# Attention into two MoE layers on one core: queries and keys in longer runs, one merged chain, a later fourth weight sum

## The chip, the cores and the metric

The kernel runs on one core of a Trainium2 chip. The metric is device time in microseconds (us). TensorE (PE in the profile) multiplies matrices; VectorE (DVE), ScalarE (ACT) and GpSimd (POOL) work on rows of elements; SyncE (SP) issues transfers, which 16 DMA engines carry out. Each engine works through its own list of instructions in order, and semaphores hold it where another engine's result is needed.

## What is computed

Attention of 4 batches, 8 heads, 576 tokens of 64 elements: a mean-pooled attention (four tokens to one, result repeated four times) plus a local one in which a token sees only its neighbours at a distance below 4. The 2304 tokens of 512 then go through two layers of an expert with 2048 inner units.

```python
def _attn_ref(q, k, v):                    # q, k, v: [4, 8, 576, 64]
    q_d = q.reshape(B, H, Sd, factor, D).mean(axis=3)          # factor 4; k_d, v_d too
    out_up = np.repeat(sm_attn(q_d, k_d, v_d), factor, axis=2)
    mask = np.abs(pos[:, None] - pos[None, :]) < factor
    scores = np.where(mask, scale * q @ k.T, -1e9)
    out_local = softmax(scores) @ v
    return out_up + out_local

def _moe_ref(x, w_in, w_out):              # [2304,512], [512,2048], [2048,512]
    h = x @ w_in
    return np.maximum(0.01 * h, h) @ w_out

def _moe2_ref(x, w_in, w_out):             # same shapes
    h = x @ w_in                           # 0 below -1, h above 1, (h+1)**2/4 between
    g = np.where(h >= 1, h, np.where(h <= -1, 0, (h + 1) ** 2 / 4))
    return g @ w_out
```

## The kernel before

**The list planner.** The program is written as chains of operations, each with an engine, a planned duration and what it depends on. A list planner (class Issue, from L165) walks through planned time and gives each engine the ready operation of least rank, subject to free memory, free PSUM banks and each chain's due step. The result is fixed at build time: on the chip every engine works down its list and waits on semaphores. In the first 140 planned microseconds (FILL), whenever the planned TensorE has nothing ready, or the planner counts too little streamed by it of late, it places a **filler**: a matmul of zeros with 512 columns whose result nobody reads (fill(), L2301).

**Attention.** P_BLOCKS names the blocks of 64 tokens whose local attention runs on TensorE: all nine of batch 0, seven of batch 1. The others go over VectorE (local_d). For each of the four head pairs of those two batches, prep() loads q and k (L957): two DMAs each, one per head, in which one element run is a token's 64 floats (256 bytes). The tile holds 64 partitions (the token within its block) by nine blocks; TensorE transposes each block of 64x128 (L992, five blocks and then four), and ScalarE copies the transposed columns out of PSUM into qT and kT, contiguous (L1005). down() does the pooled attention (its sums over four tokens, L1079 and beside; a product on GpSimd, L1061). local_p() is the chain of the local attention: a matmul that lays the mask into PSUM (L1262, or L1268 where the piece is the last block), the scores (L1277), row maximum (DVE L1290), exp (ACT L1295), the norm (L1302, L1303, L1313), the transposes (L1320), a copy (ACT L1324), the product with v (L1337), the sum with the pooled part (DVE L1351) and its split into two f16 numbers (ACT L1361, DVE L1367). Batch 0 has pieces of 4, 4 and 1 blocks, batch 1 of 3 and 4, each for four head pairs.

**The layers.** Weights arrive as 64-bit numbers (DMAs of 512 KB and more), are rebuilt to f32 on VectorE (L628, L634, L640) and split into a high and a low f16 part (ACT L662, DVE L695); every product is three matmuls. Tokens come in four blocks of 512 and one of 256. L1698 is the first product of a block, L1961 and L1973 the second. In the second layer the last three blocks use seven products of halves in place of eight (L1727, L1897), for which sums of quarters of the weights are made: out_sums() makes four (T1 to T4) for every two slices of w_out, in one chain: VectorE sums rows of 1024 (L771), combines them at 512 (L782), ScalarE makes the high part (L802) and VectorE the low one (L805). EARLY_O says how many of these chains may run before the first layer's weight memory is handed over.

Of the kernel before, what the change touches and what calls it, by code (L numbers as in the profile page):

```python
# [9 lines left out]
F16 = mybir.dt.float16  # L10
# [20 lines left out]
LEAD_O = 4  # L31
# [6 lines left out]
FP = 2  # L38
EARLY_O = 2
# [32 lines left out]
LO_PE = (0, 0)  # L72
ADD_PE = ()
# [13 lines left out]

NORM_ACT = (1,)
# [269 lines left out]
def kernel(  # L358
# [103 lines left out]
    ident_w = const.tile([P, P], F32, name="ident_w")  # L462
    ident_n = const.tile([P, P], F16, name="ident_n")

    def consts():
# [4 lines left out]
        nc.vector.tensor_scalar_mul(ident_w, ident, SW)  # L470
        nc.vector.tensor_scalar_mul(ident_n, ident, -1.0)
# [103 lines left out]
    def weight(m, which, f, due):  # L575
# [89 lines left out]
        if m == 1 and f < LO_PE[which]:  # L665

            def low():
                ps = st["ps"] = banks.get()
                nc.tensor.matmul(ps, ident_w, st["f", f].ap, start=True, stop=False)
                nc.tensor.matmul(ps, ident_n, hi, start=False, stop=True)  # L670

            ch.op("PE", dict(dur=5 * t_mm(512), cols=5 * 512), low, banks=1, mlp=True,
                  after=free)
            w_ready[m, which, f] = ch.op(
                "ACT", t_act(512, True), lambda: nc.scalar.copy(lo, st["ps"]),
                after=(lambda: banks.put(st["ps"]),))
            ch.close()
            return
# [62 lines left out]

    FH = KFF // 2
# [10 lines left out]
    def half_sums(ch, size, row, own, steps, groups, deps, need, last=(), gate=None):  # L753
# [20 lines left out]
        for i in order:  # L774
            made[i] = ch.op(
                "DVE", t_dve(size), lambda i=i: rebuild(i, i == order[0]), deps,
                need=(size,) + (need[:1] if i == order[0] else ()))
# [78 lines left out]
    def out_sums(f, due):  # L856
        words = 3 * FP * HD
        keep = {}
        fs = range(f, f + FP)

        def make():
            b = buf(words)
            keep["a"] = b.ap.bitcast(F16).rearrange("p (j s f n) -> p j s f n", j=3, s=2, f=FP)
            for k, g in enumerate(fs):
                o_ap[g] = {nm: keep["a"][:, j, :, k] for j, nm in enumerate(("T1", "T4", "T2"))}
                o_ap[g]["T3"] = w2_out[:, :, g, HD:2 * HD]

        ch = Chain(due, LEAD_O, 4 * FP * HD)
        ch.window = WINDOW_O
        r = half_sums(  # L870
            ch, 2 * FP * HD,
            lambda i: w2_out[:, :, f + FH * (i - 1):f + FH * (i - 1) + FP], "T", T_STEPS,
            ((("11",), ("T1",), lambda s: keep["a"][:, 0, s]),
             (("21", "22"), ("T4", "T2"), lambda s: keep["a"][:, 1:3, s]),
             (("12",), ("T3",), lambda s: w2_out[:, s, f:f + FP, HD:2 * HD])),
            [w_ready[2, 1, g + k] for g in fs for k in (0, FH)], (words, make),
            [o for g in fs for o in o_after.get(g, [])], lambda: f < EARLY_O or w1_open())
        for g in fs:
            o_ready[g] = r
# [65 lines left out]
    def prep(b, hp, due):  # L945
# [6 lines left out]

        def load(nm, src):
            st[nm] = buf(QBB * P, True)
            a = st[nm].ap[:QB].rearrange("p (n h d) -> p n h d", n=QBB, h=2)
            for par in range(2):
                nc.sync.dma_start(  # L957
                    out=a[:, :, par, :],
                    in_=src[b, 2 * hp + par].rearrange("(n i) d -> i n d", i=QB),
                )  # L960
# [35 lines left out]
        def tr_c(nm, i):  # L996
# [3 lines left out]
            if i == 0:  # L1000
                t.make()
                if nm == "k":
                    nc.gpsimd.memset(t.ap[:, 0:HALO], 0.0)
                    nc.gpsimd.memset(t.ap[:, S + HALO:], 0.0)
            nc.scalar.activation(  # L1005
                out=t.ap[:, o + n0 * QB:o + n1 * QB],
                in_=st["ps", nm, i][:, :(n1 - n0) * QB],
# [1329 lines left out]
```

## Time and profile before

| | us |
|---|---|
| median of 3 runs (836.97 to 837.43) | 837.23 |
| profiled execution | 837.84 |
| its span, first to last instruction | 836.1 |
| TensorE busy | 829.8 |
| VectorE busy | 704.7 |
| ScalarE busy | 439.2 |
| GpSimd busy | 44.0 |

The profiled execution has its own time, 837.84 us; 1.74 us of it lie outside the span. A busy share is an average over stages: in the first 100 us attention and the first layer run side by side, later the layers alone. A filler counts as busy TensorE, so a busy TensorE in the first 140 us is not always useful work.

### The profile page before, as it was taken

Reading aid. Unit: us, or ns where it says so; the run is one execution under the profiler, and the core shown is the slowest. Engines: PE = TensorE matmul, PEld = TensorE weight load, DVE = VectorE, ACT = ScalarE, POOL = GpSimd, SP = SyncE. Lnnn points to the kernel's source line nnn. Section 1 sums busy time; section 2 is a strip of 40 time slices with the busy share of each in tenths; the row PEclk is TensorE's granted clock in tenths of the full one; section 3 lists DMA queues with packets and bytes.
Section 4 is the critical chain, followed back from the end, with each engine's and each line's share of the span. In section 5 each row is a group of like instructions: output and inputs, shape, how many; then the busy total and the mean of one; then the engine's idle time right before and its main releaser. Section 6 shows DMA issues by size and latency. Waiting matters only on the chain.

```text
span 836.1 us, 15212 instructions
## 1 busy us (share of the span) xinstructions
PE 829.8 (99%) x5818; PEld 501.4 (60%) x5818; DVE 704.7 (84%) x1298; ACT 439.2 (53%) x1055; POOL 44.0 (5%) x64
## 2 busy tenths in 40 slices
PE   9999999999999999999999999999999999999998
PEld 5665554444444444554444444444588888889997
DVE  4997999899999999748996989997598988867761
ACT  4888874454345334644353322344365777766650
POOL 2201000000000022100330000000000000000000
PEclk9999999999999999999999999999999999999999
DMA  7879565457640244411563030000000000000001
GB/s 141 171 180 232 175 200 208 137 165 223 224 139 2 66 111 65 94 57 58 104 118 114 1 111 3 1 1 2 1 1 1 2 1 2 26 15 13 3 14 64
DMA packets 77991, 67.82 MB, mean 81 GB/s; under 512 B 36318, under 2 KB 65374, under 8 KB 77918
## 3 DMA queue, kind: packets, MB, share of 16 engines
q1 hardware_dynamic: 66718, 62.69, 26.0%
q0 software_dynamic: 11200, 4.15, 4.5%
q8 instruction: 46, 0.75, 0.4%
q14 instruction: 27, 0.22, 0.1%
HBM read 62.08 MB, written 4.72 MB: 80 GB/s over the span
## 4 chain that ended last, share of the span: by engine, by line
PE 98%; ACT 1%; DVE 0%; issue 0%; DVEq 0%
PE bank L1698 32%; PE bank L1961 22%; PE bank L1897 11%; PE bank L1727 11%; PE bank L1973 10%; PE bank L2301 3%; PE bank L992 1%; PE bank L1277 1%; PE bank L1187 1%; PE bank L1118 1%; PE bank L1337 1%; PE bank L1169 1%; PE bank L1320 1%; PE bank L1553 1%; PE bank L1262 0%; PE bank L1102 0%
## 5 line engine op out<-in xcount | busy, mean ns | idle before, releaser
L1698 PE MATMUL bank<-arena,w 128*128 128x512 f16 (+1 forms) x1344 | 285.1, 364 | 0.0
L1698 PEld LDWEIGHTS <-w 128*128 128x128 f16 x1344 | 130.2, 98 | 135.2 <-issue 1.6
L1961 PE MATMUL bank<-arena,w 128*128 128x512 f16 (+1 forms) x816 | 181.8, 373 | 0.0
L1961 PEld LDWEIGHTS <-w 128*128 128x128 f16 x960 | 93.1, 98 | 88.2 <-issue 0.2
L1810 ACT ACTIVATE arena<-bank 128x512 f32<-128x512 f32 x64 | 38.1, 595 | 97.8 <-PE bank L1698 92.4
L1973 PE MATMUL bank<-w,arena 128*128 128x512 f16 x384 | 88.2, 379 | 0.0
L1940 DVE SCALAR_TENSOR_TENSOR arena<-arena 128x512 f16<-128x512 f32 x96 | 66.0, 687 | 22.3 <-ACT arena L1936 22.0
L1936 ACT ACTIVATE arena<-arena 128x512 f16<-128x512 f32 x96 | 60.4, 630 | 36.9 <-DVE arena L1822 33.6
L1973 PEld LDWEIGHTS <-arena 128*128 128x128 f16 x384 | 36.8, 98 | 43.2 <-issue 1.2
L1897 PEld LDWEIGHTS <-w 128*128 128x128 f16 x516 | 50.3, 98 | 5.7
L1727 PEld LDWEIGHTS <-w 128*128 128x128 f16 x576 | 48.8, 98 | 4.4
L1814 ACT ACTIVATE arena<-bank,half 128x512 f32<-128x512 f32 x36 | 24.7, 687 | 42.2 <-PE bank L1698 38.5
L1547 DVE TENSOR_TENSOR arena<-arena 128x768 f32<-128x768 f32 (+2 forms) x60 | 41.2, 688 | 1.4
L662 ACT ACTIVATE w<-arena 128x512 f16<-128x512 f32 x34 | 21.3, 627 | 37.0 <-DVE arena L640 36.8
L1472 DVE TENSOR_TENSOR arena<-arena 128x1792 f32<-128x1792 f32 x20 | 40.3, 2019 | 0.3 <-issue 0.3
L1517 DVE TENSOR_TENSOR arena<-arena 128x1792 f32<-128x1792 f32 x20 | 40.3, 2017 | 0.0
L1480 DVE TENSOR_REDUCE arena<-arena 128x28 f32<-128x1792 f32 x20 | 40.2, 2013 | 0.1
L1727 PEld LDWEIGHTS <-arena 128*128 128x128 f16 x432 | 36.7, 98 | 5.3 <-issue 1.9
L1897 PE MATMUL bank<-w,w 128*128 128x256 f16 x300 | 38.6, 273 | 0.0
L1822 DVE SCALAR_TENSOR_TENSOR arena<-arena,bank 128x512 f32<-128x512 f32 x36 | 24.6, 683 | 16.5 <-ACT arena L1818 16.4
L1822 DVE SCALAR_TENSOR_TENSOR w<-w,bank 128x512 f32<-128x512 f32 x36 | 24.6, 684 | 14.4 <-ACT w L1818 14.1
L1727 PE MATMUL bank<-w,w 128*128 128x128 f16 (+1 forms) x384 | 35.9, 246 | 0.0
(199 smaller groups left out, 1290.2 us busy)
## 6 DMA issues: line engine op xcount, KB each, us to landing
arena<-in_moe_w_in_dram SPq DMA_DIRECT2D x18, 512.0 KB
arena<-in_moe_w_out_dram SPq DMA_DIRECT2D x17, 512.0 KB
w<-in_moe_w_out_dram SPq DMA_DIRECT2D x15, 512.0 KB
arena<-in_moe_w_in_dram SPq DMA_DIRECT2D x4, 1024.0 KB
w<-in_moe_w_in_dram SPq DMA_DIRECT2D x3, 1024.0 KB
arena<-in_k_dram SPq DMA_DIRECT2D x23, 112.0 KB
arena<-in_v_dram SPq DMA_DIRECT2D x23, 112.0 KB
out_dram<-arena SPq DMA_DIRECT2D x10, 256.0 KB
```

The lines of the kernel that those rows point to most:

```text
L1472: nc.vector.tensor_tensor(pv(par, j0), st["q", par].ap.rearrange("p (j d) -> p j d", d=D)[:, j0:j0 + JC, :] .unsqueeze(2).to_broadcast([P, ...
L1480: nc.vector.reduce_sum(sv(par)[:, j0:j0 + JC, :], pv(par, j0), axis=AX)
L1517: nc.vector.tensor_tensor(pv(par, j0), window(st["v", par], j0, JC), sv(par)[:, j0:j0 + JC, :].unsqueeze(3).to_broadcast([P, JC, W, D]), o ...
L1547: nc.vector.tensor_tensor(out, x, y, op=ALU.add)
L1698: nc.tensor.matmul(h[:, e], a[:, f, c, :], y[:, :, c, :], start=(n == 0), stop=(n == 3 * KDM - 1),)
L1727: nc.tensor.matmul(o[:, e], a[:, i, c], y[:, k, c, :], start=first and e == 0 and n == 0, stop=n == 5, skip_group_check=True,)
L1822: nc.vector.scalar_tensor_tensor(out=t, in0=t, scalar=1.0 / s_in, in1=st["h", p], op0=ALU.min, op1=ALU.max)
L1897: nc.tensor.matmul(o[:, k], a[:, i, at:at + P], y[:, j], start=opens and p == e == k == n == 0, stop=p == PH - 1 and e == E - 1 and n == 2 ...
L1936: nc.scalar.activation(out=gv(p)[0], in_=st["t", p].ap, func=AF.Copy, scale=so)
L1940: nc.vector.scalar_tensor_tensor(out=lo, in0=st["t", p].ap, scalar=so, in1=hi, op0=ALU.mult, op1=ALU.subtract)
L1961: nc.tensor.matmul(o, a, y[:, e, :], start=(first and n == 0 and c % E == 0), stop=(last and n == 2), skip_group_check=True,)
L1973: nc.tensor.matmul(st["acc"][tt], a, y[:, f, :], start=(first and n == 0), stop=(last and n == 2),)
```

## The change

Line numbers of the changed kernel stand in brackets.

- **q and k of batches 0 and 1** (TURN): one DMA loads q or k of a head pair [L1040]. Partition i holds tokens 9i to 9i+8 of each head, one run of 2304 bytes. 32 transfers of 144 KB become 16 of 288 KB. GpSimd copies the tile into the order that the transposes read [L1049], in two parts of 5 and 4 blocks (64 partitions by 640 and 512 floats). A transposed block n now holds tokens n, n+9, n+18, ..., so ScalarE's copy out of PSUM [L1102] writes with a step of nine floats (36 bytes). The planned costs of the load are smaller, and 1.3 us of GpSimd are planned per q or k.
- **Batch 0's last block:** four chains of one block (one per head pair) become one chain of four; it needs one mask matmul, one row maximum, one norm, one copy and so on, over four blocks' columns.
- **w_out's sums:** out_sums makes T1, T2 and T3 in one chain [L883, L891, L894, L921, L923] and T4 in a second one that is due eight steps later [L934, L944, L946, L948]. EARLY_O goes from 2 to 4 (two chains may run early instead of one), and memory is set aside for the coming x2 pairs when a chain starts (Kept).
- Paths that were switched off (LO_PE, ADD_PE) and two constants that only they used (ident_w, ident_n) are gone.

The planner then places everything anew, as order shows. There are 61 fillers in place of 86: 16 in place of 18 ahead of the first transposes, 45 in place of 68 after that. The layers' matmuls are the same.

GpSimd ahead of its first product for the pooled attention; w_61 is the memory of the early work, L1003 and L1004 clear the edges of kT. Before:

```order
L486 MEMSET arena 128x3
L487 MEMSET arena 128x3
L967 MEMSET w_61 3x64
L1003 MEMSET w_61 128x3
L1004 MEMSET w_61 128x3
L1061 TENSOR_TENSOR w_61<-w_61 72x4x128
```

After:

```order
L1059 MEMSET w_61 3x64
L1049 COPY w_61<-w_61 64x2x5x64 x2
L1049 COPY w_61<-w_61 64x2x4x64
L1049 COPY w_61<-w_61 64x2x5x64
L1095 MEMSET w_61 128x3
L1096 MEMSET w_61 128x3
L1049 COPY w_61<-w_61 64x2x4x64
L1049 COPY w_61<-w_61 64x2x5x64
L1049 COPY w_61<-w_61 64x2x4x64 x2
```

The copies of the first two head pairs stand ahead of the first product; 32 of them are on GpSimd's list in all.

TensorE, the last block of batch 0 (L1268 is its mask, L1277 its scores). Before, two of the four chains:

```order
L1268 LDWEIGHTS ident_72
L1268 MATMUL bank_70<-band,ident_72 128x70
L1277 MATMUL bank_70<-w_61 64x70 x2
L1187 MATMUL bank_69<-w_61 64x144 x4
L1320 MATMUL bank_66<-ident,w_61 70x128 x4
L1268 LDWEIGHTS ident_72
L1268 MATMUL bank_64<-band,ident_72 128x70
L1277 MATMUL bank_64<-w_61 64x70 x2
```

After, all four head pairs under one mask (scores at L1386):

```order
L1381 LDWEIGHTS ident_72
L1381 MATMUL bank_68<-band,ident_72 128x280
L1386 MATMUL bank_68<-w_61 64x70 x4
L1386 MATMUL bank_68<-arena,w_61 64x70 x2
L1386 MATMUL bank_68<-w_61 64x70 x2
L2402 LDWEIGHTS zeros
L2402 MATMUL bank_63<-zeros 128x512
L1290 MATMUL bank_64<-arena,w_61 64x144 x4
```

Three masks with their weight loads are gone, and one bank is in use where four were.

TensorE, transposes of five blocks of a q or k of batch 1 beside the first layer (L992, now L1084). Before, at about 78 us, fillers (L2301) stand around them:

```order
L2301 MATMUL bank_67<-zeros 128x512
L992 MATMUL bank_67<-ident,w_61 128x64 x5
L1169 MATMUL bank_63<-ident,w_61 72x72 x4
L2301 LDWEIGHTS zeros
L2301 MATMUL bank_65<-zeros 128x512
```

After, matmuls of the layer (L1797 was L1698, L2060 was L1961) stand around them:

```order
L1797 MATMUL bank_63<-arena,w_79 128x512
L1429 MATMUL bank_67<-ident,w_61 70x128 x4
L1084 MATMUL bank_69<-ident,arena 128x64 x5
L2060 LDWEIGHTS w_79
L2060 MATMUL bank_68<-arena,w_79 128x512
```

The diff, cut to its core:

```diff
-EARLY_O = 2
+T4_LATE = 8.0
+KEEP = 2
+EARLY_O = 4
...
+RUSH_M = 8.0
+TURN = (0, 1)
+T_LOAD = 0.7
+L_LOAD = 1.2
+T_TURN = 1.3
...
     def out_sums(f, due):
...
+        ch = Chain(due, LEAD_O, 3 * n)
+        a = ch.op("DVE", t_dve(2 * n), row, [w_ready[2, 1, g + k] for g in fs for k in (0, FH)],
+                  need=Kept((2 * n, 2 * n, n)))
+        b = ch.op("DVE", t_dve(n), last_q, [a], need=(n,))
+        t1 = ch.op("DVE", t_dve(n), lambda: minus(lambda: r(0), lambda: r(1), lambda: r(0)), [a])
+        t3 = ch.op("DVE", t_dve(n), lambda: minus(lambda: r(1), q22, lambda: r(1)), [b, t1])
+        t2 = ch.op("DVE", t_dve(n), lambda: minus(q22, q22, lambda: r(0)), [t3])
...
+        ch = Chain(due + T4_LATE, LEAD_O, 2 * n)
+        o = ch.op("DVE", t_dve(2 * n), diff, [ready["T2"]], need=Kept((n, 2 * n)))
...
         def load(nm, src):
...
+            st["r", nm] = buf(QBB * P, True)
+            nc.sync.dma_start(
+                out=st["r", nm].ap[:QB].rearrange("p (h x) -> p h x", h=2),
+                in_=src[b, 2 * hp:2 * hp + 2].rearrange("h (i n) d -> i h (n d)", n=QBB),
+            )
+
+        def turn(nm, i):
+            n0, n1 = ((0, NA), (NA, QBB))[i]
+            if not i:
+                st[nm] = buf(QBB * P, True)
+            nc.gpsimd.tensor_copy(
+                st[nm].ap[:QB].rearrange("p (n h d) -> p h n d", n=QBB, h=2)[:, :, n0:n1],
+                st["r", nm].ap[:QB].rearrange("p (h n d) -> p h n d", n=QBB, h=2)[:, :, n0:n1],
+            )
...
+            to = t.ap[:, o:o + S]
+            if runs:
+                to = to.rearrange("p (i n) -> p n i", n=QBB)[:, n0:n1]
             nc.scalar.activation(
-                out=t.ap[:, o + n0 * QB:o + n1 * QB],
-                in_=st["ps", nm, i][:, :(n1 - n0) * QB],
+                out=to,
+                in_=st["ps", nm, i][:, :(n1 - n0) * QB].rearrange("p (n i) -> p n i", i=QB),
                 func=AF.Copy, scale=0.125 if nm == "q" else 1.0,
             )
...
-    def local_p(b, n0, cnt, hp, due):
+    def local_p(b, n0, cnt, hps, due):
...
+        cells = [(hp, n0 + i) for hp in hps for i in range(cnt)]
...
+            if nh > 1:
+                e = edges(n0)
+                mask = band[:, e:e + 1, :].to_broadcast([P, nc_, KB])
...
-                if pb == b:
+                one = cnt == 1
+                if pb == b and (not one or hp == NHP - 1):
                     due = first[1, block_at(b * S + n0 * QB)]
-                    local_p(b, n0, cnt, hp, max(at_hp, due - HP_GAP * NHP) + 0.05 * n0)
+                    local_p(b, n0, cnt, list(range(NHP)) if one else [hp],
+                            max(at_hp, due - HP_GAP * NHP) + 0.05 * n0)
```

## Rows read from the trace of the kernel before

**Rows 1.** The page: busy us (share of the span) and instructions of each engine.

```profile
PE 829.8 (99%) x5818; PEld 501.4 (60%) x5818; DVE 704.7 (84%) x1298; ACT 439.2 (53%) x1055; POOL 44.0 (5%) x64
```

**Rows 2.** Waits of TensorE: line waited for, us in total, times, longest us.

```profile
PE bank L1727 <- DVE w L1822: 1.1, 1, 1.1
PE bank L1727 <- ACT arena L1759: 0.5, 1, 0.5
```

**Rows 3.** All fillers: duration min/median/max ns, first and last start us.

```profile
L2301 PE MATMUL bank<-zeros x86: 377/385/634, 1.2 to 101.9; 128*128 128x512 bf16 x86
```

**Rows 4.** Timeline of TensorE: start us, us, what, count; three groups of fillers.

```profile
1.20 6.95 PE L2301 MATMUL bank<-zeros 128*128 128x512 bf16 x18 [1.20 <-DVE half L468]
8.79 1.47 PE L2301 MATMUL bank<-zeros 128*128 128x512 bf16 x6
10.19 0.77 PE L992 MATMUL bank<-ident,w 64*128 64x64 f32 x9
76.39 1.46 PE L2301 MATMUL bank<-zeros 128*128 128x512 bf16 x6
```

**Rows 5.** Same timeline: single-block and four-block chains of batch 0.

```profile
11.76 0.28 PE L1262 MATMUL bank<-band,ident 128*128 128x280 bf16 x1
12.62 0.78 PE L992 MATMUL bank<-ident,w 64*128 64x64 f32 x9
16.61 0.20 PE L1268 MATMUL bank<-band,ident 128*128 128x70 bf16 x1
17.02 0.60 PE L2301 MATMUL bank<-zeros 128*128 128x512 bf16 x2
29.28 0.69 PE L1337 MATMUL bank<-w 70*64 70x64 f32 x16
29.90 0.39 PE L2301 MATMUL bank<-zeros 128*128 128x512 bf16 x1
51.52 0.34 PE L1337 MATMUL bank<-w 70*64 70x64 f32 x4
51.78 0.46 PE L992 MATMUL bank<-ident,arena 64*128 64x64 f32 x4
```

**Rows 6.** Windows: from:to us, length, busy us (instructions) by engine, PEclk, DMA share, GB/s.

```profile
5.00:7.00 2.00, 2.00 (x6) 0.76 (x5) 0.47 (x8) 0.00 (x0) 0.00 (x0) 1.00 1.21 192
20.00:80.00 60.00, 60.00 (x666) 38.07 (x663) 51.91 (x153) 52.63 (x220) 8.45 (x16) 1.00 0.89 186
220.00:240.00 20.00, 20.00 (x94) 9.11 (x93) 20.00 (x32) 8.36 (x14) 0.00 (x0) 1.00 0.78 260
580.00:600.00 20.00, 20.00 (x97) 9.19 (x96) 9.39 (x14) 6.46 (x11) 0.00 (x0) 1.00 0.00 1
```

**Rows 7.** GpSimd by line and shape: count | busy us, mean ns | idle before, releasers.

```profile
L1061 POOL TENSOR_TENSOR w<-w 72x512 f32<-72x512 f32 x4 | 5.2, 1298 | 9.8 <-PE bank L1277 7.9 <-DMA w<-in_v_dram 1.9
L478 POOL TENSOR_SCALAR_AFFINE_SELECT arena<-arena 64x420 f32<-64x420 f32 x2 | 1.2, 599 | 0.1
L475 POOL MEMSET arena<- 128x420 f32 x1 | 0.4, 448 | 0.0
```

**Rows 8.** Timeline of GpSimd: the last of its constants; start us, us.

```profile
4.39 0.10 POOL L487 MEMSET arena<- 128x3 f32 x1
```

**Rows 9.** ScalarE by line and shape, columns as in rows 7.

```profile
L1005 ACT ACTIVATE w<-bank 128x320 f32<-128x320 f32 x16 | 6.9, 440 | 12.1 <-PE bank L992 11.2 <-POOL w L1004 0.8
L1005 ACT ACTIVATE w<-bank 128x256 f32<-128x256 f32 x16 | 6.2, 386 | 0.3 <-PE bank L992 0.3
L1574 ACT ACTIVATE arena<-arena 128x512 f16<-128x512 f32 x10 | 6.3, 630 | 6.0 <-DVE arena L1567 6.0
L1936 ACT ACTIVATE w<-w 128x512 f16<-128x512 f32 x6 | 3.8, 626 | 0.1
```

**Rows 10.** VectorE by line and shape, columns as in rows 7.

```profile
L782 DVE TENSOR_TENSOR arena<-arena 128x512 f32<-128x512 f32 x27 | 18.0, 686 | 0.1
L771 DVE TENSOR_TENSOR arena<-w 128x1024 f32<-128x1024 f16 x13 | 15.6, 1220 | 1.2 <-PE bank L1961 1.2
```

More of the change, by code (lines that the diff above doesn't have):

```diff
@@ L664, in weight @@
         free = (lambda: st["f", f].free(),)
[L665 to L678, printed above, removed]
         if LO_DMA[m][0] <= f < LO_DMA[m][1]:
@@ L732, in __bool__, with __init__, __iter__ @@
             return True
+    class Kept:
+        def __init__(self, words):
+            self.words = words
+        def __iter__(self):
+            yield from self.words
+            for b, e in enumerate(x2):
+                if not e.made and sch.step + KEEP > step_of[1, b, KFF // per_step(b) - 1]:
+                    yield e.s.words
+        def __bool__(self):
+            return True
     FH = KFF // 2
@@ L870, in out_sums @@
[L870 to L877, printed above, removed]
+            st["r"] = buf(2 * n)
@@ new lines, in out_sums, with row_free @@
+        left = [2]
+        def row_free():
+            left[0] -= 1
+            if not left[0]:
+                st["r"].free()
+        old = [o for g in fs for o in o_after.get(g, [])]
+        ready = {}
+        for nm, o, src, dst, free in (
+            ("T1", [t1], lambda: r(0), lambda: made(0), row_free),
+            ("T2", [t2], q22, lambda: made(1), lambda: st["q"].free()),
+            ("T3", [t3] + old, lambda: r(1), lambda: quarter(0, 1), row_free),
+        ):
+            h = ch.op("ACT", t_act(n), lambda src=src, dst=dst: nc.scalar.activation(
+                out=dst()[:, 0], in_=src(), func=AF.Copy), o)
+            ready[nm] = ch.op("DVE", t_dve(n), lambda src=src, dst=dst: nc.vector.tensor_tensor(
+                dst()[:, 1], src(), dst()[:, 0], op=ALU.subtract), [h, t2], after=(free,))
@@ new lines, in out_sums @@
+        ch = Chain(due + T4_LATE, LEAD_O, 2 * n)
+        ch.window = WINDOW_O
+        o = ch.op("DVE", t_dve(2 * n), diff, [ready["T2"]], need=Kept((n, 2 * n)))
+        ch.op("DVE", t_dve(n), lambda: nc.vector.tensor_tensor(
+            d()[:, 0], d()[:, 0], d()[:, 1], op=ALU.add))
+        ch.op("ACT", t_act(n), lambda: nc.scalar.activation(
+            out=keep["t"][:, 0], in_=d()[:, 0], func=AF.Copy))
+        ready["T4"] = ch.op("DVE", t_dve(n), lambda: nc.vector.tensor_tensor(
+            keep["t"][:, 1], d()[:, 0], keep["t"][:, 0], op=ALU.subtract),
+            after=(lambda: st["d"].free(),))
@@ L878, in out_sums @@
+        ch.close()
         for g in fs:
-            o_ready[g] = r
+            o_ready[g] = ready
     def token_sums(b, due):
@@ L1305, in norm @@
         def norm():
-            sm = st["ml"].ap[:, cnt:2 * cnt]
+            sm = st["ml"].ap[:, nc_:2 * nc_]
             if b in NORM_ACT:
-                for n in range(cnt):
+                for n in range(nc_):
                     nc.scalar.activation(
```

229 lines of the change are left out of this document (128 added, 101 removed).

## The prediction

> **What bounds the kernel now.** I read the page's busy line first: TensorE is busy 829.8 of 836.1 us [rows 1], so time can only come from TensorE having less to do or waiting less. Its waits come next: those past the start are 1.1 and 0.5 us, both at the first halves' products of the second layer [rows 2]; 1.6 us is all that a shorter chain of VectorE or ScalarE could give back there. What is left is work that nobody needs. The third view lists the fillers: 86 matmuls of zeros, the first at 1.2, the last at 101.9 us [rows 3]. In the timeline 18 of them fill the start while the first loads come in, and later ones stand in groups, six from 8.79 until the transposes at 10.19, six more from 76.39 [rows 4]. They are where attention on ScalarE, VectorE and the DMA engines does not keep up with TensorE in the planner's count. So the first 100 us are bound by the feeding of TensorE and the rest by TensorE itself. What the change is worth is therefore read from TensorE's list: what it no longer has to run, less the new waits.
>
> **What goes from TensorE's list.** The changed list has 61 fillers. A filler of a group costs (10.19 - 8.79) / 6 = 0.233 us from start to start [rows 4]. The 18 at the start are dearer, 6.95 / 18 = 0.39 on average [rows 4]; two of those go, the last ones, which stand nearest to the group at 8.79, so I price all alike (0.3 more otherwise). 25 x 0.23 = **5.75 us**.
>
> The merged block: a single-block chain's mask and scores take 17.02 - 16.61 = 0.41 us, four of them 1.64; the same for four blocks takes 12.62 - 11.76 = 0.86 [rows 5]. That is 0.78 less. The product with v takes 51.78 - 51.52 = 0.26, four times 1.04, against 29.90 - 29.28 = 0.62 for four blocks [rows 5]: 0.42 less. The transposes are as many as before. Together 1.2; laying the new list out with the times from start to start of the old one gives 1.1, since neighbours change too, and I take **1.1 us**. The sum on TensorE is **6.85 us**. All layer matmuls stay, at the same shapes and rate.
>
> **Who feeds TensorE, and can they do it 6.9 us earlier?** The fillers went because the planner, with its new costs, sees useful work ready in their place. That holds on the chip only if every feeder keeps up.
>
> The DMA engines: between 20 and 80 us they are busy 0.89 of the time at 186 GB/s [rows 6]. Where only q and k come in, in 256-byte runs, a share of 1.21 goes with 192 GB/s; weights, in long runs, move 260 GB/s with 0.78 [rows 6]. Per byte that is 0.0063 against 0.0030, a factor of 2.1. The q and k of two batches are 16 loads of 295 KB, 4.72 MB: 4.72e6 x 1.21 / 192e9 = 29.7 us of all engines before, 4.72e6 x 0.78 / 260e9 = 14.2 after, if 2304-byte runs cost like the weights'. 15.5 us less in a stretch whose share leaves about 0.11 x 60 = 6.6 us: the transfers get out of the way, and weights can land earlier. At no gain at all from long runs the DMA engines would be as full as before (rival B).
>
> GpSimd gets 32 copies, and TensorE waits for them. No row shows a copy there. The nearest is the select on 64x420, one input and one output, 599 ns [rows 7]; for 640 and 512 elements at the same rate 0.91 and 0.73 us, 1.64 for a load. Below it lies a memset without input, 448 ns for 420 [rows 7], 0.68 and 0.55; above it the product of two inputs, 1298 ns for 512 [rows 7], 1.62 and 1.30, 2.92 for a load. I take the select, which moves as many elements per element written as a copy does. GpSimd is done with its constants at 4.5 us [rows 8], when q of the first head pair is in; the first eight copies then end at 4.5 + 4 x 1.64 = 11.1. TensorE's new list, counted along with the old times from start to start, reaches the parts at 7.7 (first part of q) to 16.3 us (last part of the second k), and each stands at least 2 us ahead. GpSimd is busy only 8.45 of 60 us from 20 to 80 [rows 6]; 12 loads x 1.64 = 20 us fit there. Behind the copies on GpSimd stand the clearing of kT's edges and the pooled product, and TensorE's transposes wait for the latter: at the select's price, in time. Cost **0**; with the two-input price 2.0 us (rival A).
>
> At L1061 the trace has GpSimd's two-input product at 1298 ns for 512 elements, VectorE a two-input operation of 512 at 686 ns [rows 7, 10]. [...]
>
> ScalarE: between 20 and 80 us it is busy 52.63 of 60 [rows 6], so 7.4 are spare. If that work has 6.9 us less time, 0.5 stay. The merge takes six operations from it (three copies, three scalings; column totals stay); an operation's fixed part is 440 - 320 x (440 - 386) / 64 = 170 ns [rows 9], so 1.0 us comes back: 1.5 spare. Its copies of q and k now write with a step of 36 bytes. No row has that step. The nearest strided write puts a float16 pair apart (L1574, runs of 8 bytes every 16): 630 ns against 626 for a contiguous one [rows 9], no cost. That is the low end, and I take it, as the only row with a gap in what ScalarE writes. An element costs 54 / 64 = 0.84 ns [rows 9], so half a cycle more for each of 16 x 576 is 3.9 us, less 1.5 spare: +2.4 us. A whole cycle more: 7.7 - 1.5 = +6.2. These are the high end (rival C).
>
> VectorE: 51.91 of 60 us there [rows 6], 8.1 spare less 6.9, plus what the merge takes off, of eighteen small operations. Cost 0, with little slack.
>
> **The w_out sums** lie far behind, from about 580 us on. Old chain by rows: two sums of 1024, four of 512, the low parts of 512, 1024 and 512: 2 x 1.22 + 4 x 0.69 + 0.69 + 1.22 + 0.69 = 7.8 us [rows 10]. New: one of 1024 and seven of 512, 6.05, and for T4 one and two, 2.6: 0.85 more for each, which VectorE covers where it is idle 10.6 of 20 us, from 580 to 600 [rows 6]. T1 to T3 are ready 1.75 us earlier, T4 later. What waits at L1727 today (1.6 us [rows 2]) may vanish or double; I take 0 with -1.6 and +1.6 as bounds. The dropped constants ran before TensorE's first useful work: 0. The tail behind the last matmul is unchanged: 0.
>
> **Sum.** 837.84 - 6.85 = 831.0 for the profiled execution; that one lies 0.61 above the median of 837.23, so for the median 837.23 - 6.85 = **830.4**.
>
> **Rivals.**
> A, GpSimd's copies cost the two-input price. The first four loads end at 4.5 + 11.7 = 16.2 us, where TensorE's list reaches the later parts 0.5 to 1.3 us sooner, and up to 2.0 sooner with the third head pair. For it: VectorE and GpSimd run side by side, and no copy is in the trace. Against: the select. 830.4 + 2.0 = **832.4**.
> B, the fillers come back as waits. They stood where the planner saw nothing ready; if it is VectorE's and ScalarE's chains that hold attention up (both over 0.86 busy from 20 to 80) and not the transfers, TensorE waits where it filled. For it: those shares. Against: where the planner saw work ready in the old list, TensorE hardly waited [rows 2], so its durations hold, and operations did go (the merge). 837.2 - 1.1 and some new waits: **about 837**, no change.
> C, slower. ScalarE's copies with 36-byte steps cost three cycles an element in the stretch where it is fullest: 2 x 7.7 = 15.4, less 1.5 spare, +13.9 us: **844.3**. It decides from 1 + (6.9 + 1.5) / 7.7 = 2.1 cycles an element; below that the change still gains. For it: every element lies in a place of its own. Against: the 16-byte step of L1574, which costs nothing.
> [...]
>
> **Chances.** Forecast 0.77, A 0.08, B 0.06, C 0.09, of which 0.07 end slower than now and 0.02 between. A measurement of this kernel can tell about 0.2% (1.7 us) from no change. Faster: 0.77 + 0.08 + 0.02 = 0.87; same 0.06; slower 0.07. The range goes from 828.4 (the waits at L1727 vanish, and a little more from the copies) to 833.5 (A, or half a cycle at C, or L1727's waits doubled, with 1 us of lost slack); B and the worse part of C, 0.15, lie outside.
>
> **What would show it.** GpSimd's copies at about 0.9 and 0.7 us, and no wait of TensorE on them; L1102 at 440 and 386 ns as L1005 had; 61 fillers; TensorE at the place of 150 us some 6.8 us ahead, and the same lead at the end; the wait list still below 2 us. I am wrong if waits of TensorE appear before 105 us, if the DMA share from 20 to 80 us stays near 0.89 while weights come late, or if the second layer's waits grow beyond 3 us.

## The result: slower, with TensorE's clock at half rate for a stretch

The changed kernel takes 846.78 us (median of four runs, 841.69 to 850.24) against 837.1: a ratio of 1.0112, interval 1.0077 to 1.0146. The forecast was 830.4 us, with a range up to 833.5. The mean granted clock, as a share of full speed, is 0.992 in the run of 841.69 us, 0.985 and 0.986 in those of 846.73 and 846.83, and 0.984 in that of 850.24. The kernel before has 0.999 or 1.000 in nearly all its runs.

The page of the profiled run (841.69 us): span, busy line, clock row, chain by engine.

```profile
span 839.9 us, 15106 instructions
...
PE 831.7 (99%) x5790; PEld 501.9 (60%) x5790; DVE 709.1 (84%) x1286; ACT 446.3 (53%) x1053; POOL 67.0 (8%) x96
...
PEclk9969999999999999999999999999999999999999
...
PE 92%; DVE 6%; ACT 1%; issue 0%; DVEq 0%; ACTq 0%
```

TensorE is as busy as in [rows 1], but a busy engine at half rate hides in that number. The third slice of the clock row shows it. The windows of the same run (from:to, length, busy us of TensorE, weight loads, VectorE, ScalarE, GpSimd, granted clock, DMA share, GB/s):

```profile
38.00:40.00 2.00, 1.80 (x28) 1.29 (x24) 1.93 (x7) 1.47 (x11) 1.34 (x3) 1.00 1.14 221
40.00:42.00 2.00, 1.58 (x16) 1.25 (x17) 1.93 (x8) 2.00 (x9) 0.84 (x2) 1.00 1.11 209
42.00:44.00 2.00, 2.00 (x17) 1.31 (x14) 2.00 (x5) 2.00 (x8) 1.38 (x1) 0.71 0.99 378
44.00:56.00 12.00, 12.00 (x102) 7.58 (x100) 8.45 (x16) 7.10 (x21) 3.17 (x9) 0.50 0.55 137
56.00:58.00 2.00, 2.00 (x30) 1.26 (x30) 1.56 (x5) 1.92 (x9) 0.39 (x2) 0.88 0.65 136
```

Up to 42 us the granted clock is 1.00; between 38 and 42 TensorE is busy 3.38 of 4 us. From 44 to 56 us the clock is 0.50. Lost by it, as an estimate (length times the share of the clock that is missing): 2 x 0.29 + 12 x 0.50 + 2 x 0.12 = 6.8 us.

What stands ahead of the fall, on the timelines of TensorE, VectorE and GpSimd:

```profile
39.35 0.44 PE L1272 MATMUL bank<-ident,w 72*72 72x72 f32 x4
40.42 0.63 PE L1429 MATMUL bank<-ident,w 128*70 128x128 f32 x4 [0.63 <-DVE w L1422]
...
36.53 1.59 POOL L1049 COPY arena<-w 64x640 f32<-64x640 f32 x1
...
37.45 0.69 DVE L1411 TENSOR_SCALAR w<-w 128x4 f32<-128x4 f32 x1
38.18 0.18 DVE L1412 RECIPROCAL w<-w 128x4 f32<-128x4 f32 x1
...
39.78 0.59 DVE L1422 TENSOR_TENSOR w<-w 128x280 f32<-128x280 f32 x1
```

TensorE waits 0.63 us for a norm (L1422). That norm is late because an add over four columns (L1411), which takes 0.16 us at 33.25, with GpSimd idle, took 0.69: it ends at 38.14, when GpSimd's copy ends (36.53 + 1.59 = 38.12). VectorE then has no idle time until the norm is done, so the 0.53 us of the add reach it, and the norm itself takes 0.59 in place of 0.44.

TensorE's waits in this run, then GpSimd's and ScalarE's rows for the new work (those of [rows 2, 7, 9] answer to them):

```profile
PE bank L1826 <- DVE w L1921: 2.2, 2, 1.1
PE bank L1429 <- DVE w L1422: 0.6, 1, 0.6
PE bank L1826 <- DVE bank L1869: 0.3, 1, 0.3
...
L1049 POOL COPY w<-w 64x640 f32<-64x640 f32 x6 | 4.5, 757 | 2.0 <-DMA w<-in_k_dram 1.6 <-DMA w<-in_q_dram 0.4
L1049 POOL COPY arena<-w 64x512 f32<-64x512 f32 x5 | 4.7, 942 | 0.0
L1049 POOL COPY w<-arena 64x640 f32<-64x640 f32 x1 | 1.5, 1524 | 1.8 <-DVE w L1422 1.8
...
L1102 ACT ACTIVATE w<-bank 128x320 f32<-128x320 f32 x12 | 9.1, 760 | 7.0 <-PE bank L1084 7.0
L1102 ACT ACTIVATE w<-bank 128x256 f32<-128x256 f32 x12 | 7.7, 641 | 0.5 <-PE bank L1084 0.5
```

The copies cost 0.60 us (at 8.30) and 0.71 (at 7.57) while VectorE is idle, and up to 1.59 beside VectorE (at 36.53). ScalarE's writes with a step of 36 bytes take 760 and 641 ns instead of 440 and 386.

Laid along the old start-to-start times, as in the prediction, the new list is 0.2 us late at 39 us, 1.0 after the wait at 40.4, 7.5 at 56.4, 9.4 at 160, and 12.55 at the end; the old list is late by 1.86 at its end. This run is 10.7 us longer than the 831.0 that the old profiled time less the shorter list would give (841.69 - 831.0, and 12.55 - 1.86): some 6.5 for the clock, 2.9 of other lateness in the first 160 us and 1.3 for longer waits at the first halves' products. Of the 2.9, wait rows of TensorE show 0.63 and 0.24; where the rest arises is open. The median run misses the forecast by 16.4. No trace shows the three longer runs, but a mean clock of 0.985 over 845 us means at most 0.015 x 845 = 12.7 us lost at half rate (an estimate; the same reckoning gives 6.7 for the profiled run), so most of the spread of the four runs is the clock's.

### The profile page after: what moved, and what is told of

It is laid out like the page before. It is cut to its first block, busy times and chain, and to the rows that moved or that the text cites. A ratio compares the mean times of both kernels' runs of the same rounds, so it can differ in the third digit from the quotient of the medians.

```text
span 839.9 us, 15106 instructions
## 1 busy us (share of the span) xinstructions
PE 831.7 (99%) x5790; PEld 501.9 (60%) x5790; DVE 709.1 (84%) x1286; ACT 446.3 (53%) x1053; POOL 67.0 (8%) x96
## 3 DMA queue, kind: packets, MB, share of 16 engines
q1 hardware_dynamic: 50078, 62.69, 25.8%
## 4 chain that ended last, share of the span: by engine, by line
PE 92%; DVE 6%; ACT 1%; issue 0%; DVEq 0%; ACTq 0%
PE bank L1797 31%; PE bank L2060 22%; PE bank L1996 10%; PE bank L2072 10%; PE bank L1826 10%; PE bank L2402 2%; PE bank L1084 1%; PE bank L1290 1%; PE bank L1272 1%; PE bank L1386 1%; PE bank L1221 1%; PE bank L1441 1%; PE bank L1429 1%; PE bank L1652 1%; DVE w L1182 0%
## 5 line engine op out<-in xcount | busy, mean ns | idle before, releaser
L1797 PE MATMUL bank<-arena,w 128*128 128x512 f16 (+1 forms) x1344 | 285.3, 364 | 0.2 <-DVE w L682 0.2
L1797 PEld LDWEIGHTS <-w 128*128 128x128 f16 x1344 | 129.9, 98 | 134.3 <-issue 1.6
L2060 PE MATMUL bank<-arena,w 128*128 128x512 f16 x768 | 176.4, 380 | 0.0
L2060 PEld LDWEIGHTS <-w 128*128 128x128 f16 x960 | 92.6, 98 | 88.9 <-issue 1.2
L1909 ACT ACTIVATE arena<-bank 128x512 f32<-128x512 f32 x64 | 37.9, 592 | 91.9 <-PE bank L1797 87.0
L1826 PEld LDWEIGHTS <-w 128*128 128x128 f16 x684 | 57.8, 98 | 7.2 <-issue 1.9
L1996 PEld LDWEIGHTS <-w 128*128 128x128 f16 x480 | 46.8, 98 | 5.4
L1826 PE MATMUL bank<-arena,w 128*128 128x256 f16 x336 | 41.3, 273 | 1.4 <-DVE w L1921 1.1
L1646 DVE TENSOR_TENSOR arena<-arena 128x768 f32<-128x768 f32 (+2 forms) x60 | 41.3, 689 | 1.5
L1913 ACT ACTIVATE w<-bank,half 128x512 f32<-128x512 f32 x38 | 26.0, 685 | 19.2 <-DVE bank L1876 15.1
L1996 PE MATMUL bank<-w,w 128*128 128x256 f16 x288 | 36.0, 273 | 0.0
```

What stands on the lines that cost most here:

```text
L1646: nc.vector.tensor_tensor(out, x, y, op=ALU.add)
L1797: nc.tensor.matmul(h[:, e], a[:, f, c, :], y[:, :, c, :], start=(n == 0), stop=(n == 3 * KDM - 1),)
L1826: nc.tensor.matmul(o[:, e], a[:, i, c], y[:, k, c, :], start=first and e == 0 and n == 0, stop=n == 5, skip_group_check=True,)
L1913: nc.scalar.activation(out=t, in_=st["h", p], func=AF.Relu, scale=0.5 * s_in, bias=half)
L1996: nc.tensor.matmul(o[:, k], a[:, i, at:at + P], y[:, j], start=opens and p == e == k == n == 0, stop=p == PH - 1 and e == E - 1 and n == 2 ...
L2060: nc.tensor.matmul(o, a, y[:, e, :], start=(first and n == 0 and c % E == 0), stop=(last and n == 2), skip_group_check=True,)
```

## The experiments

Theory 1: ScalarE's slower copies feed TensorE late, and the clock falls after the wait. Theory 2: the list is too thin for the clock whatever feeds it. Theory 3: GpSimd's copies make TensorE late. The time of the kernel before has a median between 837.26 and 837.42 beside each of them.

**1. ScalarE without the step** (e1_plain_write).

```diff
-                to = to.rearrange("p (i n) -> p n i", n=QBB)[:, n0:n1]
+                to = to.rearrange("p (n i) -> p n i", i=QB)[:, n0:n1]
```

> The changed kernel with ScalarE's copies of q and k written without a step (the tokens stay in the order in which the transposes leave them, so the undoing of the permutation is left out); every engine's list is otherwise the same. Theory 1 (late feeding: the strided copies, 760 and 641 ns where they took 440 and 386, and the copies on GpSimd make TensorE wait, and after the wait its clock falls): the copies are back at 440 and 386 ns, ScalarE has 9.2 us less to do, the waits near 40 us shrink or go, the clock stays at full rate, about 832 to 834 us. Theory 2 (thin list: with 25 fillers fewer TensorE streams too little for its clock, whoever feeds it): the clock falls all the same near 40 us, 840 us or more. Theory 3 (GpSimd's copies hold VectorE up, and ScalarE matters little): the wait on VectorE's norm near 40 us stays, and with it the fall, 840 or more; it is told from theory 2 by the next kernel.

Measured: 844.32 us, ratio 1.0079 (1.0045 to 1.0113). The copies are back at 436 and 389 ns, TensorE waits 1.35 us for the norm (L1422) at 41.3, and the clock falls all the same; a window, columns as above:

```profile
40.00:60.00 20.00, 17.46 (x167) 11.97 (x172) 15.20 (x37) 12.24 (x46) 6.71 (x12) 0.66 0.61 155
```

Theory 1 is out. Two of its ten runs kept the full clock (1.000), at 837.69 and 838.28: even without a fall this kernel is no faster than the one before, which is not the forecast either.

**2. No copies on GpSimd** (e2_no_copy).

```diff
-            nc.gpsimd.tensor_copy(
...
-            a = st[nm].ap[:QB].rearrange("p (n c) -> p n c", n=QBB)
+            a = (st["r", nm] if runs else st[nm]).ap[:QB].rearrange("p (n c) -> p n c", n=QBB)
```

> The changed kernel without the 32 copies on GpSimd: the transposes read the loaded tile as it lies, so the layout of the blocks is left out of the computation; strided writes on ScalarE stay, the planned durations too, and the list of TensorE is the same but for memory names and 24 matmuls of the first layer. Theory 1: ScalarE's strided copies stay at 760 and 641 ns, so part of the lateness stays; between 833 and 842 us. Theory 2: the clock falls all the same, 840 or more. Theory 3: VectorE's small operations are no longer held (the add ahead of the reciprocal at 0.16 us and not 0.7 to 1.3), no wait near 40 us, the clock holds: 832 to 834 us.

**3. Both** (e3_no_copy_plain: both diffs).

> Both: no copies on GpSimd and no step in ScalarE's writes (layout and order of the tokens are left out). Theories 1 and 3: the clock holds at full rate and the time is that of the forecast, 830.4 to 832 us. Theory 2: the clock falls, 838 us or more, though nothing feeds TensorE late.

Measured: 835.49 us (0.9979, 0.9969 to 0.9988) and 836.21 (0.9996, 0.998 to 1.0012). The clock of experiment 2 in the same window:

```profile
40.00:60.00 20.00, 19.24 (x218) 12.51 (x219) 19.24 (x52) 18.66 (x71) 2.66 (x4) 1.00 0.97 205
```

The clock holds with the same thin list in all ten runs of experiment 2 (0.999 or 1.000), so theory 2 in its plain form is out, and in this plan GpSimd's copies are what brings the fall about. ScalarE's step costs nothing that can be measured here (three of the ten runs of experiment 3 took 838.7 to 840.7, with a mean clock of 0.998 or 0.999). One sign of theory 3 did not come as expected: GpSimd's remaining product still holds an add of VectorE twice (1.05 us from 15.25, 1.02 from 32.15), without a fall.

But 835.5 is not 830.4. Along the old times this list is late by 1.0 us at 51, 2.6 at 86, 3.5 at 150 and 6.6 at the end: 837.4 - 6.85 + 3.5 + (6.6 - 3.5 - 1.86) = 835.3. This sorts the lateness into an early and a late part; it is read from the same run and tests nothing. Where the early 3.5 us arise is not shown. Some idle rows of 0.16 to 0.25 us in this trace are not waits: they stand where matmul records of fillers are missing, 51 of them against 61 weight loads.

```profile
L2402 PEld LDWEIGHTS <-zeros x61: 95/98/151, 1.2 to 87.2; 128*128 128x128 bf16 x61
L2402 PE MATMUL bank<-zeros x51: 379/390/634, 1.2 to 87.2; 128*128 128x512 bf16 x51
```

**4. Sixteen more fillers** (e4_two_fill).

```diff
-            nc.tensor.matmul(ps, zeros[:, 0:P], zeros, start=True, stop=True)
+            for _ in range(2 if 22 < t < 46 else 1):
+                nc.tensor.matmul(ps, zeros[:, 0:P], zeros, start=True, stop=True)
```

> The changed kernel with each filler that the plan puts between 22 and 46 us issued twice: 16 more matmuls of zeros, 3.7 us of TensorE, everything else in the same order. Theory 2: the clock holds, 13.6 us at half rate go and 3.7 come, about 838 us or less, and repeated runs agree. Theories 1 and 3: the fillers also stand in for waits, so the sum rises by less than 3.7; if the waits are what lets the clock fall it may hold here as well, and if they stay it falls: 841 to 846 us. The sharper sign is the granted clock between 40 and 60 us with and without a wait ahead of it.

Measured: 839.47 us (1.0033, 1.002 to 1.0045). In eight of ten runs the clock is full (1.000); two at 842.9 and 843.5 have 0.993. The profiled run:

```profile
17.02 0.60 PE L1429 MATMUL bank<-ident,w 128*70 128x128 f32 x4 [0.56 <-DVE w L1422]
...
41.90 0.63 PE L1429 MATMUL bank<-ident,w 128*70 128x128 f32 x4
...
40.00:60.00 20.00, 19.37 (x237) 12.73 (x237) 18.36 (x48) 16.45 (x61) 9.58 (x15) 1.00 0.83 201
```

The add is still held by GpSimd's copy (38.54 + 0.69 = 39.23 against 37.70 + 1.51 = 39.21), but the transposes behind the late norm start at 41.90 without a wait; the waits on L1422 of this run stand at 17.0 and 19.0 us. So the fillers took away the wait together with the thin list, and this experiment does not tell the two apart. That a wait alone is not enough, the changed kernel itself shows, among the second layer's products of 256 columns, where the clock stays at 1.00 behind a wait of 1.11 us:

```profile
687.18 4.75 PE L1826 MATMUL bank<-arena,w 128*128 128x256 f16 x42 [1.11 <-DVE w L1921]
...
686.00:688.00 2.00, 0.89 (x9) 0.73 (x8) 1.89 (x5) 1.13 (x4) 0.00 (x0) 1.00 0.00 0
688.00:690.00 2.00, 2.00 (x20) 1.79 (x19) 2.00 (x6) 1.68 (x4) 0.00 (x0) 1.00 0.00 0
```

**5. The kernel before with 18 fillers left out** (b_thin).

```diff
-            nc.tensor.matmul(ps, zeros[:, 0:P], zeros, start=True, stop=True)
+            if not 22 < t < 46:
+                nc.tensor.matmul(ps, zeros[:, 0:P], zeros, start=True, stop=True)
```

> The kernel before with the 18 fillers left out that the plan puts between 22 and 46 us; everything else in the same order, no copies on GpSimd, no step in ScalarE's writes. If fillers only stand in for waits, TensorE waits where they stood and the time is 837.4 us or up to 4 less. If they also hold the clock, it falls in that stretch here too and the time is 841 us or more; then a thin stretch is enough and the copies are only one way to it.

Measured: 845.21 us (1.0089, 1.0062 to 1.0117), with no copy on GpSimd and no step. The window of the kernel before, then the same of this one:

```profile
40.00:60.00 20.00, 20.00 (x242) 13.29 (x239) 18.84 (x62) 16.71 (x70) 1.65 (x5) 1.00 0.82 190
40.00:60.00 20.00, 18.85 (x201) 13.40 (x202) 15.96 (x52) 13.88 (x57) 1.65 (x5) 0.74 0.65 152
```

TensorE waits in five pieces of 0.2 to 0.5 us (1.55 of the 8 us from 38 to 46) before the clock falls, and all five runs have a mean clock of 0.982 to 0.994. The fillers were not spare: with these matmuls that nobody reads the window has a clock of 1.00, and where their place turned into waits, 0.74.

**6. The kernel before with as many copies on GpSimd, read by nobody** (b_copies).

```diff
+    scratch = const.tile([P, P], F32, name="scratch")
...
             for n in range(n0, n1):
+                nc.gpsimd.tensor_copy(scratch[:QB], a[:, n, :])
                 nc.tensor.transpose(
```

> The kernel before with 144 copies of 64x128 floats on GpSimd (one for each block of q and k of batches 0 and 1, as much as the change copies there) into a scratch tile that nobody reads; the transposes do not wait for them, the two unused constants give the scratch its place. Theory 3 (GpSimd's copies hold VectorE's operations up, and TensorE waits for the norms that come late): VectorE's add ahead of the reciprocal (L1302 of the kernel before, one line on here) takes up to a microsecond, TensorE gets waits of 2 to 5 us in the first 100 us, 839 to 843 us, with or without a fall of the clock. If it is only the wait of the transposes for their copies that counts: 837.4 us, no change.

Measured: 841.32 us (1.0053, 1.0038 to 1.0068), clock 1.00. The copies cost 4.0 us without a fall and without any transpose waiting for them. The way is not the one expected: the add of L1302 took 0.274 us at most. TensorE's waits (one line further down in this kernel):

```profile
PE bank L1699 <- DVE w L695: 1.9, 1, 1.9
PE bank L1278 <- POOL w L1005: 1.6, 3, 0.8
```

L1005 clears the edges of kT: 0.15 us of work (mean of 8) that now stands behind copies on GpSimd's list, and the scores wait for it. L695 is the low part of the first layer's weights, late on VectorE. The two make 3.5 of the 4.0 us. In small pieces (386 ns for 64x128) these copies kept GpSimd busy for over 52 us, twice the 26 of the change, so the 4.0 us is not the price of the change itself.

**7. No adds ahead of the reciprocals**, in the changed kernel (a_no_add) and in the one before (b_no_add).

```diff
-            nc.vector.tensor_scalar_add(sm, sm, 1e-9)
             nc.vector.reciprocal(sm, sm)
```

> The changed kernel without the adds of 1e-9 ahead of the reciprocals on VectorE (the sums are at least 1, where the add changes no f32 number): these are the operations that GpSimd's copies held up most, to 0.7 and 1.3 us where they take 0.16 alone. All other lists are the same. Theory 3: VectorE's norms come earlier, the wait near 40 us goes, the clock holds in most runs, 834 to 838 us. If another operation takes the delay over in their place, or the thin list alone lets the clock fall: 842 to 847 us as with the adds.

> The kernel before without the same adds: VectorE has 43 small operations less, some 7 us, but TensorE sets the end and the fillers stay: 837.4 us, at most 1 us less. It is the measure for the kernel above, so that what the adds themselves cost is not put down to the copies.

Measured: 837.47 us (1.001, 0.9998 to 1.0021) against 846.78 with the adds; 837.25 (0.9999, 0.999 to 1.0008) for the kernel before. So 43 small operations on VectorE cost 9 us in one kernel, and 46 cost nothing in the other. Without them no wait of TensorE stands ahead of 66 us, and the mean granted clock of the ten runs is 0.998 or more. The hold itself went over to other operations in part: the norm (L1422) took 1.28 us at 30.69 and 0.70 at 39.59, in place of 0.44. So the edit shows that the adds' time on VectorE led to the wait near 40 us; it does not separate the time that GpSimd added from the adds' own. The profiled run (840.37) shows the other way in which a copy makes TensorE late, and behind that wait, at 66.7 us, the clock falls here too, for about 3 us, worth 1.7:

```profile
PE bank L1084 <- POOL arena L1049: 2.6, 1, 2.6
...
68.00:70.00 2.00, 2.00 (x6) 0.76 (x5) 2.00 (x5) 0.79 (x2) 0.68 (x1) 0.50 1.11 210
```

**8. Part by part.** Old loads (p1_turn_off), the w_out sums alone (p6_sums_only), no merge (p3_no_merge), and a dearer plan price for the copies (h1_turn2):

```diff
-TURN = (0, 1)
+TURN = ()
...
-                one = cnt == 1
+                one = False
...
-T_TURN = 1.3
+T_TURN = 2.2
```

The first diff alone is p1, the first two p6, the second p3, the third h1.

> The changed kernel with q and k loaded as before (TURN empty): the merged chain and the new w_out sums stay, no copies on GpSimd, no step in ScalarE's writes. The planner puts 98 fillers in, 12 more than before; TensorE's list is 0.9 us longer than that of the kernel before by the old times. Theory A (the fall of the clock comes with GpSimd's copies; the late waits of 3.2 us where there were 1.9 come with the w_out sums): no fall, 837.4 + 0.9 + 1.3 = 839.6 us. Theory B (the late waits have another source than the sums): 838.3 us. If the clock falls here too, GpSimd's copies are not what brings it.

> The kernel before with the new w_out sums alone (TURN empty, the last block in four chains): 86 fillers, TensorE's list as long as before. Theory A: the waits at the first halves' products grow from 1.9 to about 3.2 us, 838.7 us. Theory B (the sums cost nothing): 837.4 us.

> The changed kernel with the last block of batch 0 in four chains again: 73 fillers, TensorE's list 3.4 us shorter than before, 3.4 longer than the changed kernel's. If thin streaming together with waits behind GpSimd's copies lets the clock fall, 12 more fillers make it rarer: without a fall 837.4 - 3.4 + 3.0 (waits in the first 150 us) + 1.3 = 838.3 us, with one 844. If the copies alone bring it, it falls as often as in the changed kernel, 844 to 847.

> The changed kernel with 2.2 us planned for GpSimd's copies of a q or k in place of 1.3 (a copy of five blocks takes 0.7 us alone and up to 1.6 beside VectorE): 75 fillers, TensorE's list 5.2 us shorter than before. If the planner's price for the copies is what left TensorE waiting with too little to stream, the clock holds here and the waits of the first 150 us shrink to 1 or 2 us: 837.4 - 5.2 + 1.5 + 1.3 = 835 us. If the copies hold VectorE up whatever is planned, the waits stay at 3.5 us or more and some runs show a fall: 837 to 842.

Measured: 841.09 (1.0047, 1.003 to 1.0063), 837.69 (1.0007, 0.9998 to 1.0016), 841.77 (1.0065, 1.0041 to 1.009) and 847.83 us (1.0131, 1.0087 to 1.0175). The sums alone cost nothing. With the old loads the merge is a loss: 98 fillers, and the clock holds (0.999 or 1.000); 1.5 us more than expected stand in no row. Without the merge one of four runs has a fall (846.09, clock 0.992). The other three, at 841.5 to 841.8, hold the clock (1.000); the profiled one of them is 6.2 us late after 90 us along the old times. The dearer price was my worst expectation: the planner moved everything, the waits came elsewhere (1.3 and 1.1 us for norms, 1.2 for ScalarE), and the clock fell twice in the profiled run (0.50 from 48 to 60 us, 0.80 from 180 to 190).

How long a wait is does not decide by itself in the early part either. In that run of the dearer price the clock stayed at 1.00 behind a wait of 0.81 us at 37.9 and fell behind one of 1.06 at 45.8; without the merge it stayed at 1.00 behind 1.36 us at 35.2; in the changed kernel it fell behind 0.63. What decides is not shown.

**9. What is left of the early and of the late waits**: copies for batch 0 only (g1_turn0), the old w_out sums (g3_oldsums), both (g5_turn0_oldsums), all without the adds.

```diff
-TURN = (0, 1)
+TURN = (0,)
...
-EARLY_O = 4
+EARLY_O = 2
```

In g3 and g5 out_sums and its helper are the old ones as well.

> The changed kernel without the adds of 1e-9 and with the new loads and GpSimd copies for batch 0 only (batch 1 loaded as before): 76 fillers, TensorE's list 3.6 us shorter than before, 16 copies on GpSimd, all ahead of or beside batch 0's attention. If the early waits come from copies that land beside the first layer's weights (batch 1), they shrink to about 1 us here and the clock holds: 837.3 - 3.6 + 1 + 1.3 = 836 us. If batch 0's copies bring them, 3 us or more of waits stay: 838 us or more.

> The changed kernel without the adds of 1e-9 and with the w_out sums as before (four sums in one chain, EARLY_O 2): TensorE's list is that of the changed kernel. If the late waits at the first halves' products (3.2 us in the changed kernel, 1.9 before) come from the new sums, they are 1.9 here and the time is 1.3 us below that of the kernel without the adds, 836.2 us. If the plan's shift brings them, 3.2 stay: 837.5 us.

> Both edits: copies for batch 0 only, the old w_out sums, no adds of 1e-9; 76 fillers. With both sources of waits reduced: 837.3 - 3.6 + 1 = 834.7 us, below both kernels. If either holds the waits up, 836 to 838 us.

Measured: 838.03 (1.0013, 1.0003 to 1.0022), 846.7 (1.0106, 1.0082 to 1.013) and 841.14 us (1.0058, 1.0036 to 1.0081). Copies for batch 0 alone leave TensorE 2.7 us late in the early part with the clock at 0.999 or 1.000: enough to eat the 3.6 us that the list is shorter, once the later waits are added. Both expectations on the sums fell. With the old ones TensorE's waits at the layers' products are far longer, in g3:

```profile
PE bank L1925 <- ACT arena L1891: 3.4, 1, 3.4
PE bank L1755 <- DVE bank L1798: 2.3, 1, 2.3
PE bank L1925 <- DVE arena L1895: 1.4, 2, 1.1
PE bank L1755 <- DVE w L1850: 1.1, 1, 1.1
```

Behind the wait of 3.4 us the clock falls as well (0.50 from 710 to 712 us, 0.70 to 714, worth 1.7 us), and in g5 behind one of 2.4 (0.50 from 624 to 626, 0.66 to 628). With the new sums such waits come to 2.5 us (a_no_add). They are a gain within this change.

**10. The layout on TensorE** (k1_two_heads), without the adds as well (k2_two_heads_no_add), and with the doubled products in the plan (k4_two_heads_pe).

```diff
+            a = st["r", nm].ap[:QB].rearrange("p (h n d) -> p h n d", h=2, n=QBB)
...
+                    for par in range(2):
+                        nc.tensor.matmul(
+                            ps[par * D:(par + 1) * D, c], a[:, par, n, :], ident[:QB, :QB],
+                            start=True, stop=True,
+                        )
```

> The changed kernel without GpSimd's copies and with the computation whole: each block is transposed straight from the loaded tile by two products with the identity, one per head (64x64 each, into the two halves of the bank), in place of one transpose of both heads. Sixteen 64x64 products of this kind take 0.69 us in L1337's row, so eighteen cost about what nine transposes did (0.77). The plan is the one that gave 835.5 us without copies. If GpSimd's copies are the cause of the miss, 835 to 837 us with the clock held, below the kernel before; if the doubled products lengthen the early waits, 838 or more.

> The same without the adds of 1e-9 on VectorE: if VectorE's small operations still set some of the early waits of 3.5 us, 833.5 to 835 us; if not, the time of the kernel above.

> As the first of the three, but the planner counts the doubled products at twice the transposes' columns and time: it puts 51 fillers in and moves useful work, so TensorE's list is some 2 us shorter. If fillers stand where TensorE would wait anyway, the time is that of the first, 835 to 837 us; if the list counts, 833.5 to 835; if 51 are too few to hold the clock, 841 or more.

Measured: 841.65 (1.005, 1.0035 to 1.0065), 841.61 (1.0049, 1.0034 to 1.0064) and 841.08 us (1.0057, 1.0034 to 1.0079). Rows of k1, the products of five blocks, and a window:

```profile
6.05 0.80 PE L1087 MATMUL bank<-ident,w 64*64 64x64 f32 x20
...
40.00:60.00 20.00, 20.00 (x340) 14.22 (x341) 17.56 (x49) 17.47 (x67) 2.63 (x4) 1.00 0.85 213
```

I had misread the count: such a product shows as two records, so five blocks cost 0.80 where five transposes take 0.52, four 0.68 in place of 0.46, and sixteen loads 16 x (0.28 + 0.22) = 8.0 us. In this whole kernel without copies on GpSimd no wait between the start and 680 us is listed and the clock holds; but the doubled products fill TensorE's time too, so it is experiment 2 that tests the copies alone. The price is higher than expected: 837.4 - 6.85 + 8.0 + 1.3 = 839.9, and 1.8 us of the 841.65 have no row. No whole kernel here beats the one before.

## Why the prediction was wrong

**The list.** Right as far as the count goes: 61 fillers. What the shorter list is worth no run measured by itself; the nearest, experiment 2 and k1, are 5 and, after the doubled products and the late waits are counted, 1.8 us above what it would give. The step that failed is the one behind it, that fillers are work which nobody needs. Here they held the clock: without 18 of them it fell from 1.00 to 0.74 between 40 and 60 us, and the kernel before went from 837.3 to 845.21 us (experiment 5). The prediction named the price of the start's slow fillers and asked no further what the 23 others did for the rate of what stood between them. No rival had the fall.

**GpSimd's own price.** 0.71 and 0.60 us against 0.91 and 0.73 taken: the select was the right row and even a little dear, and rival A, at 1.62 and 1.30, is out. What was left out is what VectorE pays beside it. A row of the kernel before had it:

```profile
14.33 1.26 POOL L1061 TENSOR_TENSOR w<-w 72x512 f32<-72x512 f32 x1 [5.64 <-PE bank L1277]
...
14.85 0.78 DVE L1302 TENSOR_SCALAR w<-w 128x4 f32<-128x4 f32 x1
```

An add of 0.16 us took 0.78 and ended (15.63) with GpSimd's product (15.59). I priced what the work costs GpSimd, and put what it costs VectorE beside it at nothing. In the changed kernel VectorE's add took 0.69 us beside GpSimd's copy, in place of 0.16, and ended with it (38.14 and 38.12). Why the one is held beside the other no run here shows.

**VectorE, "cost 0, with little slack".** This is the second step that failed, and where the first came due: a delay of 0.53 us on VectorE reached TensorE as a wait of 0.63, and behind that wait, in a stretch with fewer fillers, some 6.8 us were lost at a clock of 0.50. Without the copies the clock held (experiment 2), and with 18 fillers fewer it fell without any copy (experiment 5).

**ScalarE.** The step costs (760 - 440) / 320 = 1.0 ns an element, 1.2 times the 0.84 ns that an element took before [rows 9] and that the prediction counts as a cycle: 2.2 in all, just above the 2.1 from which rival C would decide, and far from the low end that I took. Yet without the step the time is the same (836.21 against 835.49). The spare that I worked out, busy time over a stretch, was no measure of what waits: the equal times say that no wait that counts hung on these copies.

**The DMA engines.** The 15.5 us did not come. Shares of 16 engines over the span, before and then after:

```profile
q1 hardware_dynamic: 66718, 62.69, 26.0%
```

```profile
q1 hardware_dynamic: 50078, 62.69, 25.8%
```

26.0% of 836.1 is 217.4 us, 25.8% of 839.9 is 216.7: 0.7 us less for 16,640 packets fewer. No run shows that the time hung on it.

**Rival B** was right in kind and too weak: the time of the fillers did come back as lateness, 3.5 us without the copies, of the 5.75 that they were worth, though hardly any of it stands in rows of waits. **The w_out sums** at 0 with bounds of 1.6: late waits grew by 1.3, within the bounds, and not through the sums.

What stays open: what makes TensorE late in the first 150 us. It was 0 to 1.3 us late with the old loads, 2.7 to 6.2 with the new ones and the clock held; no single edit removed this but for the layout on TensorE, which fills the time itself. Why the copies of b_copies made the low part of the weights late (1.9 us) is not shown either.

## What to carry to other kernels

Before counting filler work as a gain, ask what it does to the clock: leave the fillers out of the old kernel once and read the granted clock of that stretch. Work moved to an idle engine is priced on its neighbours too; look in the trace for their short operations that end together with its long ones. And when a static plan is changed, waits come back elsewhere: a list that is 6.9 us shorter gave 1.9 at best, in a kernel that leaves the layout out.

## What the runs showed of the hardware

- In the changed kernel the granted clock fell from 1.00 to 0.50 behind a wait of 0.63 us, with TensorE busy 3.38 of the 4 us ahead with transposes and small products, and was 0.50 from 44 to 56 us, through 12 us of unbroken work of the same kind. Among products of 256 columns a wait of 1.11 us left it at 1.00. With sixteen matmuls of 512 columns more in the early stretch it held (1.00) in eight of ten runs; with 18 such matmuls fewer, in the kernel before, it fell to 0.74 from 40 to 60 us in place of 1.00.
- VectorE's add over 128x4 (0.16 us with GpSimd idle) took 0.24 to 1.30 us beside an operation on GpSimd, and ended 0.02 to 0.11 us after it; GpSimd's copy of 64x640 took 0.71 us with VectorE idle and up to 1.59 beside VectorE.
- ScalarE writing f32 with a step of 36 bytes took 760 ns for 320 columns in place of 440, 1.0 ns an element more; writing f16 in 8-byte runs every 16 bytes it took 630 ns for 512 columns, against 626 without the gaps [rows 9].
- Runs of 2304 bytes in place of 256 left the busy time of the DMA engines as it was (26.0% and 25.8% of the span).
- An f32 product of 64x64 showed as two matmul records (twenty for ten products in k1) and a transpose as one (five for five blocks in the changed kernel), and matmul records were missing from a trace (51 beside 61 weight loads in experiment 2).
